# Attention and MLP kernel: one split for the last queries' transposes, the row sums' guard and reciprocal after their transpose

## The chip, the cores and the metric

One core of a Trainium2 chip runs the whole program. The metric is device microseconds (us) of that core. The kernel before took 748.15 us, the median of three runs (747.27 to 751.06 us).

## The reference

The inputs are q, k, v of 4 batches, 8 heads, 576 positions and 64 channels, a small MLP that gives a position bias, and the weights of a two-layer MLP. Cut to what matters:

```python
scores = scale * np.matmul(q, k.transpose(0, 1, 3, 2)) + bias
attn = np.exp(scores - np.max(scores, axis=-1, keepdims=True))
attn = attn / (np.sum(attn, axis=-1, keepdims=True) + 1e-09)
x = np.matmul(attn, v)                       # then to (2304, 512)
h = x @ w_in                                 # 512 -> 2048
g = np.where(h >= 1, h, np.where(h <= -1, 0, (h + 1) ** 2 / 4))
out = g @ w_out                              # 2048 -> 512
```

All is float32. The kernel gets this from TensorE by splitting each operand into a rounded part ("hi", or h) and the rest ("lo", or l), and multiplying the parts.

## The kernel before

The program has three stages: the bias table (to about 69 us in the trace), the attention (to about 349 us) and the MLP. Both edits lie in the attention.

The attention goes over 16 head pairs n = 0 to 15 (4 pairs of heads times 4 batches). Each pair has five blocks of queries, k = 0 to 4. Blocks 0 to 3 hold 128 queries for each of the two heads j; block 4, called L, holds the last 64 queries of both heads, stacked on the 128 partitions. For a block and head, TensorE makes the scores S (L455, L456; for L: L476, L477) into one of two PSUM buffers, VectorE adds the bias and finds the row's extreme in one custom operation (`e<-S,bias`, L458, for L: L478), and ScalarE takes the exponential and sums it into a column of the 128x9 tile `sum` (L465, L484).

Then `transposes` (L521, for L: L526) turns e with TensorE, 4 pieces into a PSUM bank T, and `split` writes hi and lo of it: ScalarE casts T to hi (L496) and VectorE subtracts (L497), or, for five of the eight blocks k < 4, ScalarE copies T (L501), GpSimd or VectorE casts (L503, L505) and GpSimd subtracts (L506). Block L is split in two halves of 256 columns, one for each head, both by ScalarE and VectorE. `shared` turns the rest of the columns (T_s). `values` multiplies by v (O, L559, L561) once after block 1 and once after block 4, 20 matmuls for each, and ScalarE copies O to x. T, O and R (below) share four PSUM banks.

After block L's exponential, ScalarE adds the guard 1e-9 to `sum` (L488). The step `inv` (L672) takes VectorE's reciprocal of it, 128x9. After the second `values` of the pair, `recips` (L545) transposes it into R, 9x128, ScalarE copies it to r (L547), and SyncE stores r (L548) into a DRAM tile rT. Later `scale_x` reads xT and rT back, adds the halves (L396) and multiplies by the reciprocals (L397) on VectorE.

The work of a pair's second half lags: its second `values` and `recips` are issued between the score blocks 2 of the next pair. The order within an engine is that of the program text, rearranged by the framework's scheduler by its own estimates wherever the code does not pin an instruction (`keep`, `pool`). SyncE's queue holds all DMA issues but a few, in order.

So around R the program has, on TensorE: the 20 matmuls of O for head pair n, then R, then the scores of blocks 2 and 3 of pair n + 1 with their transposes, then S_L. On VectorE: a cast `vs` (L178), which must wait for O's last matmul since it overwrites the v tile that O reads, then `e<-S,bias` of block 2, subtractions, and `e<-S,bias` of block 3. This place is called a joint below; there is one behind each R, 15 inside the attention and one at its end.

Of the kernel before, what the change touches and what calls it, by code (L numbers as in the profile page):

```python
# [12 lines left out]
AF = mybir.ActivationFunctionType  # L13
# [8 lines left out]
P = 128  # L22
# [25 lines left out]
def attn_cpb_moe_kernel(ctx, tc, qk, vL, cb, win, wout, lw, ident, ii, out):  # L48
    nc = tc.nc
# [367 lines left out]
    with ExitStack() as ph:  # L417
# [23 lines left out]
        def scores(n, k, qkv, bias):  # L441
            qs, q0, kh, kl = qkv["q"][:, 0], qkv["q"][:, 1], qkv["k"], qkv["l"]
            if k == 0:
                sums[n] = stp.tile([P, 9], F32, tag="sum", name=f"sum{n}", bufs=3)
            later = []
            sm = sums[n]
            mx = stp.tile([P, 2], F32, tag="mx", name=f"mx{n}_{k}", bufs=6)
            if k < 4:
                e = ep.tile([P, 2 * S], F32, tag="e", name=f"e{n}_{k}")
                for j in range(2):  # L450
                    ps = psS.tile([P, 2, 512], F32, tag="S", name=f"S{n}_{k}_{j}")
                    qc = slice(P * k, P * k + P) if j == 0 else slice(704 + P * k, 704 + P * k + P)
                    for hf in range(2):
                        kc = S * j + HS * hf
                        nc.tensor.matmul(ps[:, hf, :HS], qs[:, qc], kh[:, kc : kc + HS], start=True, stop=False)  # L455
                        nc.tensor.matmul(ps[:, hf, :HS], q0[:, qc], kl[:, kc : kc + HS], start=False, stop=True)  # L456
                    ev = e[:, S * j : S * j + S]
                    nc.vector.tensor_tensor_reduce(  # L458
                        out=ev.rearrange("p (a b) -> p a b", a=2),
                        in0=ps[:, :, :HS],  # L460
                        in1=bias[k][:, S * j : S * j + S].rearrange("p (a b) -> p a b", a=2),
                        scale=-0.125, scalar=BIG, op0=ALU.add, op1=ALU.min, accum_out=mx[:, j : j + 1],
                    )
                    later.append(
                        lambda ev=ev, j=j: nc.scalar.activation(  # L465
                            ev, ev, AF.Exp, bias=mx[:, j : j + 1], scale=-1.0, accum_out=sm[:, 4 * j + k : 4 * j + k + 1]
                        )
                    )
            else:
                e = ep.tile([P, S], F32, tag="eL", name=f"e{n}_L", bufs=2)  # L470
                ps = psS.tile([P, 2, 512], F32, tag="S", name=f"S{n}_L")
                for hf in range(2):
                    for j in range(2):
                        qc = slice(512 + D * j, 640 + D * j)
                        kc = 640 * j + HS * hf
                        nc.tensor.matmul(ps[:, hf, :HS], qs[:, qc], kh[:, kc : kc + HS], start=j == 0, stop=False)  # L476
                        nc.tensor.matmul(ps[:, hf, :HS], q0[:, qc], kl[:, kc : kc + HS], start=False, stop=j == 1)  # L477
                nc.vector.tensor_tensor_reduce(  # L478
                    out=e.rearrange("p (a b) -> p a b", a=2), in0=ps[:, :, :HS],
                    in1=bias[4].rearrange("p (a b) -> p a b", a=2),  # L480
                    scale=-0.125, scalar=BIG, op0=ALU.add, op1=ALU.min, accum_out=mx[:, 0:1],
                )
                def last():
                    y = nc.scalar.activation(e, e, AF.Exp, bias=mx[:, 0:1], scale=-1.0, accum_out=sm[:, 8:9])  # L484
                    for j in range(2):
                        h_ = slice(D * j, D * j + D)
                        nc.scalar.copy(diag[n % 2][h_, h_], e[h_, 512:S])
                    nc.scalar.activation(sm, sm, AF.Identity, bias=eps_s)  # L488
                    return y

                later.append(last)
            return e, later

# [15 lines left out]
        def EV(n, k, j):  # L509
            return nc.gpsimd if (k, j) in POOL and n < LASTP else None  # L510

        def transposes(n, k, es, eT):
            hi, lo = eT
            off = P * (k % 2)
            e = es[k]
            if k < 4:
                for j in range(2):
                    ps = psT.tile([P, 4, P], F32, tag="T", name=f"T{n}_{k}_{j}")
                    for tb in range(4):
                        c0 = 640 * j + P * tb  # L520
                        nc.tensor.transpose(ps[:, tb, :], e[:, c0 : c0 + P], id_s)  # L521
                    split(ps, hi[:, 4 * j : 4 * j + 4, off : off + P], lo[:, 4 * j : 4 * j + 4, off : off + P], EV(n, k, j), (k, j))
            else:
                ps = psT.tile([P, 4, 2, D], F32, tag="T", name=f"T{n}_L")
                for tb in range(4):
                    nc.tensor.transpose(ps[:, tb].rearrange("p a b -> p (a b)"), e[:, P * tb : P * tb + P], id_s)  # L526
                for j in range(2):
                    split(ps[:, :, j, :], hi[:, 4 * j : 4 * j + 4, 256:320], lo[:, 4 * j : 4 * j + 4, 256:320], EV(n, k, j), (k, j))

        def shared(n, half, es, eT):  # L530
            hi, lo = eT
# [8 lines left out]
        def recips(n):  # L540

            p, b = n // B, n % B
            sm = sums.pop(n)
            pr = psO.tile([P, 512], F32, tag="T", name=f"R{n}")
            nc.tensor.transpose(pr[:9, :P], sm, id_s)  # L545
            r = sp.tile([9, P], F32, tag="r", name=f"r{n}")
            nc.scalar.copy(r, pr[:9, :P])  # L547
            nc.sync.dma_start(out=rT[p][b].rearrange("(k q) -> k q", q=P), in_=r)  # L548

        def values(n, half, es, eT, vs):  # L550
# [79 lines left out]
        for n in range(N):  # L630
            p, b = n // B, n % B
            if n + 2 < N:
                preps[n + 2] = prep(n + 2)
            es[n] = []
            if n >= LASTP:
                go[0] = False
            for k in range(5):
                e, later = scores(n, k, qkv[n], bias[p])
                es[n].append(e)
                exps = [False]  # L640

                def exp_():
                    if not exps[0]:
                        exps[0] = True
                        for f in later:
                            exps.append(f())

                if CFG["ex"][k] == 0:
                    exp_()
                step(2 * k)  # L650
                if p + 1 < NP:
                    for k_ in range(5):
                        if (b, k) == LB[k_]:
                            with ExitStack() as after:
                                if p == 0 and k_ in (0, 1, 4):
                                    after.enter_context(tc.issue_after(copied[2].ins))
                                bias.setdefault(p + 1, {})[k_] = load_bias(p + 1, k_)

                def tr(n=n, k=k):
                    half = k // 2 if k < 4 else 1  # L660
                    if k in (0, 2):
                        w = 256 + D * half
                        eT[n, half] = (
                            (tp0, tp1)[half].tile([P, 9, w], F32R, tag=f"hi{half}", name=f"hi{n}_{half}"),
                            (tp0, tp1)[half].tile([P, 9, w], F32R, tag=f"lo{half}", name=f"lo{n}_{half}"),
                        )
                    transposes(n, k, es[n], eT[n, half])
                    if k in (1, 4):
                        shared(n, half, es[n], eT[n, half])

                def inv(n=n):
                    nc.vector.reciprocal(out=sums[n], in_=sums[n])  # L672

                def rc(n=n):
                    recips(n)

                if k in (1, 4):
                    def av(n=n, half=0 if k == 1 else 1):
                        values(n, half, es[n], eT[n, half], qkv[n]["v"])
                    queue.append([tr, inv] if k == 4 else [tr])  # L680
                    late.append([CFG["lag"][0 if k == 1 else 1], [av] if k == 1 else [av, rc]])
                else:
                    queue.append([tr])
                while late and late[0][0] <= 0:
                    queue.append(late.pop(0)[1])
                for x in late:
                    x[0] -= 1
                drain(CFG["dr"][k], exp_, CFG["ex"][k])
                exp_()
                step(2 * k + 1)  # L690
# [415 lines left out]
```

## Time and profile before

| | |
|---|---|
| median of three runs | 748.15 us (747.27, 748.15, 751.06) |
| profiled execution | span 749.8 us (no other time of this execution is given), 13722 instructions |
| busy over the span | PE 94%, PEld 83%, DVE 72%, ACT 69%, POOL 69% |
| chain that ended last | PE 64%, DVE 6%, DMA 6%, POOL 5%, ACT 5%, issue 3% |

PE is TensorE's matmuls, PEld its weight loads, DVE VectorE, ACT ScalarE, POOL GpSimd, SP SyncE. Shares over the whole span mix three stages. The distance between two R's is the time that one head pair costs. Durations of neighbours on an engine overlap a little, so that an instruction takes somewhat less room in a row of them than its duration.

### The profile page before, as it was taken

The numbers are of one execution on the slowest core, as the hardware profiler recorded it, in microseconds if no ns is written. First come the engines' busy times: TensorE is split into PE (matmuls) and PEld (weight loads), VectorE is DVE, ScalarE is ACT, GpSimd is POOL, SyncE is SP. The second block draws the span as 40 slices with busy tenths as digits, with TensorE's granted clock in tenths as the row PEclk, the third lists the DMA queues.
The fourth block names the chain that finished last, engine by engine and source line by source line (L and its number), as shares of the span: only waits on it lengthen the run. The fifth ranks groups of instructions, "written<-read, shape, count | busy, mean of one in ns | idle before, by whom it ended". The sixth has DMA issues, their size and how long they took to land.

```text
span 749.8 us, 13722 instructions
## 1 busy us (share of the span) xinstructions
PE 703.8 (94%) x4640; PEld 621.8 (83%) x4640; DVE 537.5 (72%) x1043; ACT 518.8 (69%) x1156; POOL 519.1 (69%) x440
## 2 busy tenths in 40 slices
PE   4687999899999999989999999999999999999997
PEld 1234999888888898989988898989899988888886
DVE  7899888868898888886877776354455465666653
ACT  8896989869888998986656565344444547666563
POOL 9887778858878888871757677565656545665662
PEclk9899999989999999999999999999999999999999
DMA  8887799996997797744364645023021002000002
GB/s 228 231 271 228 200 249 240 238 234 167 233 275 192 186 271 190 177 121 162 95 199 135 197 147 163 35 83 90 7 63 32 1 1 84 1 1 1 0 1 85
DMA packets 58662, 103.37 MB, mean 138 GB/s; under 512 B 12496, under 2 KB 32736, under 8 KB 58592
## 3 DMA queue, kind: packets, MB, share of 16 engines
q1 hardware_dynamic: 56000, 92.31, 43.5%
q0 software_dynamic: 2304, 9.96, 6.4%
q8 instruction: 37, 0.61, 0.3%
q14 instruction: 33, 0.27, 0.1%
q10 hardware_dynamic: 288, 0.22, 0.1%
HBM read 67.38 MB, written 25.12 MB: 123 GB/s over the span
## 4 chain that ended last, share of the span: by engine, by line
PE 64%; DVE 6%; DMA 6%; POOL 5%; ACT 5%; issue 3%; SPq 1%; DVEq 0%; ACTq 0%; POOLq 0%
PE y L716 23%; PE h L716 16%; PE p L716 7%; PE O L559 5%; PE T L521 3%; PE S L455 3%; DMA kh<-kh 2%; PE S L456 2%; POOL lo L506 2%; DVE e L458 2%; PE O L561 1%; DMA v<-in_vL_dram 1%; ACT e L465 1%; POOL ls L136 1%; DMA x<-rT 1%
## 5 line engine op out<-in xcount | busy, mean ns | idle before, releaser
L958 POOL TENSOR_TENSOR gl<-c,gh 128x384 fp32r<-128x384 f32 x64 | 70.8, 1107 | 104.9 <-issue 87.5
L506 POOL TENSOR_TENSOR lo<-c,hi 128x512 fp32r<-128x512 f32 x75 | 101.4, 1368 | 30.2 <-DVE hi L505 27.7
L716 PE MATMUL y<-w1h,gl 128*128 128x512 f32 x288 | 114.0, 396 | 0.0
L716 PE MATMUL y<-w1l,gh 128*128 128x512 f32 x288 | 113.7, 395 | 0.0
L716 PE MATMUL y<-w1h,gh 128*128 128x512 f32 x288 | 112.0, 389 | 0.0
L465 ACT ACTIVATE e<-e,mx 128x576 f32<-128x576 f32 x128 | 100.5, 789 | 15.4 <-DVE mx L458 15.3
L458 DVE CUSTOM_DVE_ANT_0 e<-S,bias 128x576 f32<-128x576 f32 x128 | 94.4, 749 | 18.7 <-PE S L456 18.2
L455 PE MATMUL S<-kh,qa 128*128 128x288 f32 x256 | 80.0, 329 | 10.0 <-DVE mx L458 5.5
L776 ACT ACTIVATE c<-c,half_s 128x384 f32<-128x384 f32 x64 | 39.4, 615 | 60.7 <-DVE c L773 60.7
L456 PE MATMUL S<-ls,qa 128*128 128x288 f32 x256 | 73.6, 305 | 0.0
L521 PE MATMUL T<-id_s,e 128*128 128x128 f32 x512 | 71.6, 276 | 1.3 <-DVE lo L497 0.8
L982 POOL TENSOR_TENSOR gl<-c,gh 128x384 fp32r<-128x384 f32 x32 | 32.7, 1022 | 47.8 <-issue 22.3
L716 PEld LDWEIGHTS y<-w1h,gl 128*128 128x128 f32 x288 | 54.0, 187 | 11.5
L521 PEld LDWEIGHTS T<-id_s,e 128*128 128x128 f32 x512 | 59.4, 143 | 4.1 <-DVE lo L497 1.2
L455 PEld LDWEIGHTS S<-kh,qa 128*128 128x128 f32 x256 | 49.2, 192 | 15.4 <-DVE mx L458 8.8
L284 ACT ACTIVATE u<-lw,nthr 128x576 f16<-128x576 f32 (+17 forms) x104 | 57.8, 647 | 5.5 <-PE B L303 3.0
L716 PEld LDWEIGHTS y<-w1l,gh 128*128 128x128 f32 x288 | 54.0, 187 | 8.0
L716 PEld LDWEIGHTS y<-w1h,gh 128*128 128x128 f32 x288 | 54.1, 188 | 7.7
L303 PEld LDWEIGHTS <-qh 128*32 128x32 f16 x704 | 19.4, 101 | 49.4 <-issue 21.1
L286 POOL TENSOR_SCALAR u<-lw,thr 128x576 f16<-128x576 f32 (+17 forms) x36 | 51.6, 1448 | 5.0 <-PE B L303 3.8
L779 DVE TENSOR_TENSOR c<-h,c 128x384 f32<-128x384 f32 x64 | 35.4, 554 | 26.8 <-ACT c L776 26.0
L954 ACT CAST gh<-c 128x384 fp32r<-128x384 f32 x64 | 32.9, 514 | 30.5 <-DVE c L779 28.6
(266 smaller groups left out, 2112.7 us busy)
## 6 DMA issues: line engine op xcount, KB each, us to landing
bias_d<-y SPq DMA_DIRECT2D x36, 295.5 KB
qk<-in_qk_dram SPq DMA_DIRECT2D x16, 608.0 KB
qa<-in_qk_dram POOLq DMA_DIRECT2D x16, 608.0 KB, 7.2
x<-xT SPq DMA_DIRECT2D x48, 192.0 KB
raw<-in_win_dram SPq DMA_DIRECT2D x16, 512.0 KB
raw<-in_wout_dram SPq DMA_DIRECT2D x16, 512.0 KB
v<-in_vL_dram SPq DMA_DIRECT2D x16, 320.0 KB
qa<-ls SPq DMA_DIRECT2D x32, 152.0 KB
```

The lines of the kernel that those rows point to most:

```text
L284: tc.keep_in_program_order(nc.scalar.activation(u[:, :n_], lw1[:, :n_], AF.Sigmoid, bias=nthr[:, m : m + 1], scale=STEEP))
L286: EN[x].tensor_scalar(out=u[:, :n_], in0=lw1[:, :n_], scalar1=thr[:, m : m + 1], scalar2=None, op0=ALU.is_gt)
L455: nc.tensor.matmul(ps[:, hf, :HS], qs[:, qc], kh[:, kc : kc + HS], start=True, stop=False)
L456: nc.tensor.matmul(ps[:, hf, :HS], q0[:, qc], kl[:, kc : kc + HS], start=False, stop=True)
L458: nc.vector.tensor_tensor_reduce(out=ev.rearrange("p (a b) -> p a b", a=2), in0=ps[:, :, :HS], in1=bias[k][:, S * j : S * j + S].rearrange ...
L465: lambda ev=ev, j=j: nc.scalar.activation(ev, ev, AF.Exp, bias=mx[:, j : j + 1], scale=-1.0, accum_out=sm[:, 4 * j + k : 4 * j + k + 1])
L506: r = nc.gpsimd.tensor_tensor(out=lo, in0=m, in1=hi.bitcast(F32), op=ALU.subtract)
L521: nc.tensor.transpose(ps[:, tb, :], e[:, c0 : c0 + P], id_s)
L559: nc.tensor.matmul(ps[:, :w], vs[:, 4 * j + tb, :], src[:, 4 * j + tb, :], start=first and tb == 0, stop=False)
L716: a = nc.tensor.matmul(out, w, x, start=start, stop=stop)
L776: keep(nc.scalar.activation(c, c, AF.Square, scale=0.5, bias=half_s))
L958: keep(nc.gpsimd.tensor_tensor(out=gl, in0=c, in1=gh.bitcast(F32), op=ALU.subtract))
```

## The change

Block L's bank is split by one ScalarE cast and one VectorE subtraction of 512 columns in place of two each of 256. The guard is added by ScalarE in the operation that copies R out of PSUM (9x128), in place of an operation of its own on the 128x9 tile. The reciprocal is taken behind that on VectorE, of the 9x128 tile r instead of the 128x9 tile `sum`, with ScalarE's result before it and the store behind it.

```diff
-                    nc.scalar.activation(sm, sm, AF.Identity, bias=eps_s)
                     return y
...
-                for j in range(2):
-                    split(ps[:, :, j, :], hi[:, 4 * j : 4 * j + 4, 256:320], lo[:, 4 * j : 4 * j + 4, 256:320], EV(n, k, j), (k, j))
+                split(ps, *[t[:, :8, 256:320].rearrange("p (j t) d -> p t j d", j=2) for t in (hi, lo)])
...
-            nc.scalar.copy(r, pr[:9, :P])
+            nc.scalar.activation(r, pr[:9, :P], AF.Identity, bias=eps_s[:9])
+            nc.vector.reciprocal(out=r, in_=r)
             nc.sync.dma_start(out=rT[p][b].rearrange("(k q) -> k q", q=P), in_=r)
...
-                def inv(n=n):
-                    nc.vector.reciprocal(out=sums[n], in_=sums[n])
-
...
-                    queue.append([tr, inv] if k == 4 else [tr])
+                    queue.append([tr])
```

VectorE at the joint behind R of pair 8 (about 231.6 us in the trace). Before, where `a10` is a weight's bit operation (L116) and the rows run from the reciprocal of pair 8, of which three rows on are left out, to the subtractions of pair 9's block 1:

```order
L672 RECIPROCAL sum8_3509<-sum8_3509 128x9
...
L497 TENSOR_TENSOR lo8_1_3696<-T8_L_3829,hi8_1_3695 128x4x64
L497 TENSOR_TENSOR lo9_0_3848<-T9_0_0_3849,hi9_0_3847 128x4x128
L178 CAST vs10_3987<-v10_3802 128x10x64
L458 ISA e9_2_3901,mx9_2_3900<-S9_2_1_3908,bias2_2_3394 128x576
...
L116 SCALAR_TENSOR_TENSOR a10_3896<-a10_3896,raw10_3760 128x512
L458 ISA e9_3_3940,mx9_3_3939<-S9_3_0_3941,bias2_3_3433 128x576
...
L121 CAST w0h1_1495<-a10_3896 128x512
L497 TENSOR_TENSOR lo9_0_3848<-T9_1_0_3918,hi9_0_3847 128x4x128
```

The same engine and place now:

```order
L496 TENSOR_TENSOR lo9_0_3820<-T9_0_0_3821,hi9_0_3819 128x4x128
L178 CAST vs10_3960<-v10_3777 128x10x64
L458 ISA e9_2_3874,mx9_2_3873<-S9_2_1_3881,bias2_2_3373 128x576
...
L546 RECIPROCAL r8_3864<-r8_3864 9x128
L116 SCALAR_TENSOR_TENSOR a10_3869<-a10_3869,raw10_3735 128x512
L458 ISA e9_3_3913,mx9_3_3912<-S9_3_0_3914,bias2_3_3412 128x576
...
L121 CAST w0h1_1495<-a10_3869 128x512
L496 TENSOR_TENSOR lo9_0_3820<-T9_1_0_3891,hi9_0_3819 128x4x128
```

The reciprocal has moved from ahead of block 1's scores to between `e<-S,bias` of block 2 and of block 3, behind the cast `vs`; the second subtraction of T_L is gone from ahead of `vs`.

VectorE at the joint behind R of pair 11 (about 282.4 us), where `x0_2_0` is a block of attention output that is read back and scaled (L396, L397). Before:

```order
L497 TENSOR_TENSOR lo12_0_4623<-T12_0_0_4624,hi12_0_4622 128x4x128
L396 TENSOR_TENSOR x0_2_0_4504<-x0_2_0_4504 128x384
L397 TENSOR_TENSOR x0_2_0_4504<-x0_2_0_4504,xr0_2_0_4505 128x384
L178 CAST vs13_4771<-v13_4581 128x10x64
L458 ISA e12_2_4675,mx12_2_4674<-S12_2_1_4682,bias3_2_4427 128x576
...
L497 TENSOR_TENSOR lo12_0_4623<-T12_1_0_4693,hi12_0_4622 128x4x128
L497 TENSOR_TENSOR lo12_0_4623<-T12_1_1_4700,hi12_0_4622 128x4x128
L458 ISA e12_3_4724,mx12_3_4723<-S12_3_0_4725,bias3_3_4466 128x576
```

Now:

```order
L178 CAST vs13_4735<-v13_4547 128x10x64
L458 ISA e12_2_4639,mx12_2_4638<-S12_2_1_4646,bias3_2_4394 128x576
...
L546 RECIPROCAL r11_4630<-r11_4630 9x128
L396 TENSOR_TENSOR x0_2_0_4471<-x0_2_0_4471 128x384
L496 TENSOR_TENSOR lo12_0_4586<-T12_1_0_4657,hi12_0_4585 128x4x128
L397 TENSOR_TENSOR x0_2_0_4471<-x0_2_0_4471,xr0_2_0_4472 128x384
L496 TENSOR_TENSOR lo12_0_4586<-T12_1_1_4664,hi12_0_4585 128x4x128
L496 TENSOR_TENSOR lo12_0_4586<-T12_s0_4671,hi12_0_4585 128x256
L458 ISA e12_3_4688,mx12_3_4687<-S12_3_0_4689,bias3_3_4433 128x576
```

The two scaling operations have moved from ahead of `vs` to behind the reciprocal, and with one more subtraction they now stand between the scores of blocks 2 and 3. The same happens at the joints behind R of pairs 3 and 7.

## Rows read from the trace of the kernel before

**Rows 1.** The page, part 1: busy us, share of span, instructions.

```profile
PE 703.8 (94%) x4640; PEld 621.8 (83%) x4640; DVE 537.5 (72%) x1043; ACT 518.8 (69%) x1156; POOL 519.1 (69%) x440
```

**Rows 2.** Busy time by window, one head pair each, R to R.

```profile
core 0: us, PE busy (x) PEld busy (x) DVE busy (x) ACT busy (x) POOL busy (x), PEclk, DMA share, GB/s
...
231.60:249.20 17.60, 16.45 (x127) 15.51 (x125) 16.01 (x35) 15.54 (x40) 14.28 (x13) 1.00 0.73 193
```

**Rows 3.** Waits of PEld, 92 to 352 us: total us, times, longest.

```profile
PEld S L455 <- DVE mx L458: 7.3, 14, 1.6
PEld S_L L476 <- DVE mx L458: 3.8, 9, 1.4
...
PEld T L521 <- DVE lo L497: 1.2, 2, 0.6
```

**Rows 4.** Waits of DVE, 92 to 352 us.

```profile
DVE e L458 <- PE S L456: 17.6, 27, 3.2
DVE vs L178 <- PE O L561: 10.8, 11, 1.3
```

**Rows 5.** DVE by tile or line: ns min/median/max, first and last start, forms.

```profile
L257 DVE RECIPROCAL rsc<-m x1: 163/163/163, 6.6 to 6.6; 128x1 f32<-128x1 f32 x1
...
L672 DVE RECIPROCAL sum<-sum x16: 197/209/215, 89.4 to 345.5; 128x9 f32<-128x9 f32 x16
...
L497 DVE TENSOR_TENSOR lo<-T,hi x53: 673/680/694, 75.5 to 344.0; 128x512 fp32r<-128x512 f32 x53
...
L497 DVE TENSOR_TENSOR lo<-T_L,hi x32: 411/420/425, 88.6 to 346.7; 128x256 fp32r<-128x256 f32 x32
```

**Rows 6.** ACT by tile: the guard, the copy of R, the casts.

```profile
L488 ACT ACTIVATE sum<-sum,eps_s x16: 303/303/306, 84.4 to 345.2; 128x9 f32<-128x9 f32 x16
...
L547 ACT COPY r<-R x16: 250/250/251, 93.1 to 349.4; 9x128 f32<-9x128 f32 x16
...
L496 ACT CAST hi<-T x53: 559/587/610, 74.8 to 343.3; 128x512 fp32r<-128x512 f32 x53
...
L496 ACT CAST hi<-T_L x32: 348/370/389, 87.1 to 346.3; 128x256 fp32r<-128x256 f32 x32
```

**Rows 7.** DVE in order of time at pair 8's joint: start, us, idle before.

```profile
231.81 1.07 DVE L178 CAST vs<-v 128x640 fp32r<-128x640 f32 x1 [1.07 <-PE O L561]
232.80 0.74 DVE L458 CUSTOM_DVE_ANT_0 e<-S,bias 128x576 f32<-128x576 f32 x1
...
233.66 1.61 DVE L116 SCALAR_TENSOR_TENSOR a<-a,raw 128x512 int32<-128x512 int32 x1
235.19 0.74 DVE L458 CUSTOM_DVE_ANT_0 e<-S,bias 128x576 f32<-128x576 f32 x1
...
236.20 1.28 DVE L497 TENSOR_TENSOR lo<-T,hi 128x512 fp32r<-128x512 f32 x2
```

**Rows 8.** PE in order of time at the same joint.

```profile
234.24 0.60 PE L521 MATMUL T<-id_s,e 128*128 128x128 f32 x4
235.99 0.40 PE L476 MATMUL S_L<-kh,qa 128*128 128x288 f32 x1 [1.15 <-DVE mx L458]
```

**Rows 9.** DVE, then PE, in order of time at pair 11's joint.

```profile
281.56 0.77 DVE L396 TENSOR_TENSOR x<-x 128x384 f32<-128x384 f32 x1
282.36 1.73 DVE L397 TENSOR_TENSOR x<-x,xr 128x384 f32<-128x384 f32 x1
284.02 0.89 DVE L178 CAST vs<-v 128x640 fp32r<-128x640 f32 x1
284.83 0.74 DVE L458 CUSTOM_DVE_ANT_0 e<-S,bias 128x576 f32<-128x576 f32 x1
...
285.64 0.40 PE L455 MATMUL S<-kh,qa 128*128 128x288 f32 x1 [1.20 <-DVE mx L458]
```

**Rows 10.** DVE at the end of the attention.

```profile
349.85 0.56 DVE L773 TENSOR_SCALAR c<-h 128x384 f32<-128x384 f32 x1 [2.77 <-PE h L716]
```

**Rows 11.** Waits of PE, 92 to 352 us.

```profile
PE S L455 <- DMA kh<-kh: 3.4, 2, 2.0
```

## The prediction

> **What bounds the kernel now.** I read the page's busy shares first [rows 1]: TensorE's matmuls are busy for 94% of the span, VectorE, the next engine, for 72%. That is a mean over three stages, so I went to the attention, where both edits lie, and read one head pair from R to R [rows 2]. There TensorE is still ahead (16.45 of 17.60 us), but VectorE (16.01) and ScalarE (15.54) are close behind, and TensorE's granted clock is 1.00, the 2.4 GHz level. An engine that is busy 91% of a stretch can set the end wherever its work is bunched, so the next view is that of the waits. TensorE's weight loads wait for VectorE's `mx`, the result of `e<-S,bias`, 14 times at S and 9 times at S_L, together 11.1 us, and twice for a subtraction [rows 3]. VectorE for its part waits for TensorE at `vs`, 11 times and 10.8 us, because `vs` overwrites what the O matmuls read [rows 4].
>
> The two fit together in time. During O TensorE is fed and VectorE runs dry; when O ends, VectorE has a heap of work at once, and TensorE soon hangs on it. In pair 8's joint `vs` starts after 1.07 us of idling, and from there on VectorE has no gap worth naming until 236.20, while TensorE stands for 1.15 us before S_L until `e<-S,bias` of 235.19 is done [rows 7, 8]. So behind R VectorE sets the end, and in the run-up to O TensorE does.
>
> **The change part by part.** *The reciprocal.* Sixteen of 128x9 go, each 209 ns; sixteen of 9x128 come. A partition more or less is no work for VectorE that a row here shows; the elements behind each partition count, and these go from 9 to 128. One element took 163 ns, nine took 209 [rows 5]: 46 ns for 8 elements, 5.75 ns each. So 128 take 163 + 127 x 5.75 = 893 ns. Bounds: if the elements went as fast as those of a subtraction, (680 - 420) / 256 = 1.0 ns each [rows 5], it would be 163 + 130 = 293 ns; with the longest of the sixteen, (215 - 163) / 8 = 6.5 ns, 989 ns. I take 0.89 us, since both ends of its slope are reciprocals. Two subtractions in a row of 1.28 us [rows 7] against 0.68 for one show that a neighbour overlaps by 0.08 us, so the room that it takes is 0.81 us (0.21 to 0.91).
>
> The Trainium skill, "VectorE: DVE Perf Modes", the section on the fixed hardware budget in the walkthrough of the pipeline, says that the reciprocal is an iterated divide with a repeat count of 8. Eight cycles at the 0.96 GHz that the skill's first page ("Trainium Kernel Development and Optimization", Hardware Hierarchy) gives would be an estimated 8.3 ns for each element, so 1.22 us, dearer than the 5.75 ns of the rows make it; by that rule the sum below would end some 4 us higher. I go by the rows.
>
> Where it stands matters more than its size. Before, it was in the run-up to O, where the time is TensorE's. Now it stands at nearly every joint between `e<-S,bias` of block 2 and that of block 3, in the stretch in which TensorE waits for VectorE. It also waits for R and for ScalarE's copy, but `vs` and `e` occupy VectorE for 0.99 + 0.75 us behind O's end [rows 7], and R is one short matmul behind O, its copy 0.25 us [rows 6]: r is there by then, unless ScalarE is late. Behind it in VectorE's queue are subtractions that release transposes' banks, and `e` of block 3, for which S_L waits.
>
> The twelve joints without a scaling operation: full pass-through would be 0.81 us each, none would be 0. The 23 waits over 15 joints say that about each joint has one that VectorE ends, but many are short, 11.1 / 23 = 0.48 us on average, so some slack goes first; and at some joints the scheduler now puts `e` of block 3 ahead of one 0.60 us subtraction, which spares S_L what the transposes then get. I take 0.6: 12 x 0.81 x 0.6 = +5.8 us.
>
> *The three joints with scaling* (pairs 3, 7, 11). Before, L396 and L397 began during O, and `vs` could start only behind them, at 284.02; TensorE paid 1.20 us for block 2's `e` at 285.64 [rows 9]. Now `vs` does not wait for them, which gives up to 1.2 us back, but both operations stand with the reciprocal ahead of block 3's `e`, for 0.77 + 1.73 us by these rows, or some 1.5 us if the second is as short as the first. Net: +0.3 to +1.3 us beside the reciprocal; I take +0.5, nearer to the short end, since the long L397 is one row. With 0.81 each, 3 x 1.3 = +3.9 us.
>
> *The pieces that go.* On VectorE two subtractions of 420 ns become one of about 680: 0.16 us, and the old reciprocal's room, 0.13 us [rows 5]. On ScalarE the guard goes, 0.30 us, two casts of 370 become one of 587: 0.15, and the copy of R (250 ns) may grow to the guard's kind of operation, by at most 0.05 + 0.08 us from the rows' differences [rows 6]; about 0.35 us. All this lies in the run-up to O, hidden beside matmuls. If each pair gains 0.15 us of TensorE's small waits there: -2.4 us; bounds 0 and, if all of VectorE's 0.29 counts, -4.6.
>
> *Transfers.* No DMA is added. The store of r now waits for VectorE too, but the store of x's second half now goes ahead of it in SyncE's queue, so what is queued behind it (loads that are read a pair later) is delayed less than that. TensorE waits for `kh` transfers 3.4 us in two places [rows 11], and a late TensorE loses some of that: -1.3 us for the joints ahead of the longer one.
>
> *The end.* The sixteenth reciprocal stands ahead of the MLP's first clamp, where VectorE had idled for 2.77 us [rows 10]; so it can delay the clamp by no more than its room, 0.81 us, while the old one stood ahead of the last subtractions and goes. The two I set against each other.
>
> Sum: 5.8 + 3.9 - 2.4 - 1.3 = +6.0 us on the span of 749.8, so 755.8. That span is 1.65 us above the median of the runs; against the median 748.15 it gives 754.2 us.
>
> **The rivals.** *Absorbed.* VectorE's own waits, 10.8 us at `vs` and 17.6 at the scores [rows 4], show slack in each pair. If a joint passes on only 0.3 of the reciprocal, the sum is 12 x 0.24 + 3 x 0.8 - 2.4 - 1.3 = +1.6: 749.7 us, within 0.5%. For it: VectorE is busy for 16.01 of a pair's 17.60 us, so 1.6 us of it are free [rows 2]. Against it: the slack lies ahead of `vs`, the new work behind it.
>
> *Faster: the reciprocal is cheap.* If the slope is that of a subtraction, its room is 0.21 us against the 0.13 that goes; it decides if the 9x128 form takes under some 0.4 us. Then VectorE and ScalarE are both lighter in each pair by about 0.2 and 0.35 us, and with 0.28 us for each of 15 pairs the time is 748.15 - 4.2 = 744 us. For it: the two engines are near TensorE in each pair [rows 2]. Against it: 46 ns more for eight elements.
>
> *Dearer.* If an element costs half as much again as the slope (a slope from one 128x1 row is weak, since its fixed part may differ), room is 1.2 us and the nine joints' worth of pass-through (12 x 0.6 + 3 = 10.2) adds 10.2 x 0.37 = 3.8: 758 us. The skill's count of 8 named above is this case.
>
> **How the numbers follow.** Forecast 0.55, dearer 0.08, absorbed 0.25, faster 0.12. What a measurement of this kernel can tell from no change is about 0.5%, 3.7 us: between 744.4 and 751.9. The forecast's own range is 750.5 to 759, from pass-through 0.35 to 1. For 8 in 10 I go from 747.5, which takes in the absorbed case, to 761, which takes in the dearer one. Slower 0.55 + 0.08 = 0.63, same 0.25, faster 0.12.
>
> **What would show it.** Right: L546's reciprocal at 0.8 to 1.0 us; more waits of S_L and T for VectorE behind R; R to R longer by 0.3 to 0.6 us in ordinary pairs, by over 1 us in the pairs behind joints 3, 7 and 11; the MLP unchanged. Wrong: a reciprocal under 0.4 us; R to R equal or shorter although the reciprocal is long, which would put the bound elsewhere than at VectorE; or a loss in SyncE's queue (waits of L199 for r), which I have priced at nothing.

## The result and the profile after

The kernel after takes 753.53 us, the median of five runs (752.91 to 754.55), against 747.62 us for the kernel before beside it (747.27 to 751.06): a ratio of 1.0074, 95% interval 1.0056 to 1.0092. It is slower by 5.9 us in the medians; by the ratio it is 5.5 us, 4.2 to 6.9. The profiled execution of after took 754.55 us, with a span of 752.5.

The page of after, part 1 (busy us, share of the span, instructions), answers to [rows 1]:

```profile
PE 709.9 (94%) x4640; PEld 621.9 (83%) x4640; DVE 546.2 (73%) x1027; ACT 517.7 (69%) x1124; POOL 518.0 (69%) x440
```

VectorE has 16 instructions fewer and 8.7 us more. TensorE runs the same 4,640 matmuls and shows 6.1 us more busy time: a matmul that TensorE takes at a lower clock counts as busy too, so I read the loss from time stamps and not from idle time.

The operations that changed, in after, by tile: ns min/median/max, first and last start, form (compare [rows 5, 6]):

```profile
L545 ACT ACTIVATE r<-R,eps_s x16: 352/354/359, 94.2 to 352.5; 9x128 f32<-9x128 f32 x16
L546 DVE RECIPROCAL r<-r x16: 932/936/941, 94.6 to 352.8; 9x128 f32<-9x128 f32 x16
...
L495 ACT CAST hi<-T_L x16: 561/564/587, 88.4 to 348.1; 128x512 fp32r<-128x512 f32 x16
...
L496 DVE TENSOR_TENSOR lo<-T_L,hi x16: 678/692/692, 89.9 to 348.7; 128x512 fp32r<-128x512 f32 x16
```

The reciprocal takes 936 ns. Now where the time is lost. R is one matmul for each head pair, and its starts mark the pairs. Of before I take a second profiled execution here (e0, 744.9 us, span 743.1), since in the first a wait for `kh` and a granted clock of 0.58 behind it (150 to 155 us) belong to that execution alone. Rows of R by tile, of this one and of after:

```profile
L545 PE MATMUL R<-id_s,sum x16: 271/271/271, 92.7 to 342.6; 128*9 128x128 f32 x16
```

```profile
L543 PE MATMUL R<-id_s,sum x16: 271/271/271, 93.7 to 351.8; 128*9 128x128 f32 x16
```

The sixteenth R comes 9.2 us later, and behind it both need the same time (743.1 - 342.6 = 400.5; 752.5 - 351.8 = 400.7): the MLP lost nothing. Start to start of R, in us, column n is from pair n to pair n + 1 and so holds the joint behind pair n:

```
pair          0    1    2    3    4    5    6    7    8    9   10   11   12   13   14
before      15.2 16.2 16.0 17.2 17.6 17.3 16.1 17.0 17.6 17.3 16.1 17.0 17.4 18.6 13.3
after       15.5 16.9 16.7 17.9 17.9 17.3 16.2 18.0 17.9 17.3 16.2 18.0 18.5 20.1 13.7
```

This execution of before was a quick one (744.9 us against a median of 746.74 us on its chip), so the differences say where, and the medians how much.

**An ordinary joint.** VectorE of after at the joint behind pair 8, in order of time (start, us, idle before it), answers to [rows 7]:

```profile
230.33 1.30 DVE L178 CAST vs<-v 128x640 fp32r<-128x640 f32 x1 [0.97 <-PE O L560]
...
231.55 0.74 DVE L458 CUSTOM_DVE_ANT_0 e<-S,bias 128x576 f32<-128x576 f32 x1
...
232.23 0.94 DVE L546 RECIPROCAL r<-r 9x128 f32<-9x128 f32 x1
233.09 0.92 DVE L116 SCALAR_TENSOR_TENSOR a<-a,raw 128x512 int32<-128x512 int32 x1
233.94 0.74 DVE L458 CUSTOM_DVE_ANT_0 e<-S,bias 128x576 f32<-128x576 f32 x1
```

TensorE there, answers to [rows 8]:

```profile
234.75 0.41 PE L476 MATMUL S_L<-kh,qa 128*128 128x288 f32 x1 [1.16 <-DVE mx L458]
```

The reciprocal stands where the forecast put it, but block 3's `e` starts 3.61 us after `vs`, against 3.38 before: L116 took 0.92 us here and 1.61 there, and most of the reciprocal's time came out of that. The pair lost only 0.3 us.

What L116 waits out can be read from GpSimd's rows: it has a subtraction at the same time, before and after.

```profile
233.43 1.28 POOL L506 TENSOR_TENSOR lo<-c,hi 128x512 fp32r<-128x512 f32 x1
```

```profile
232.18 1.29 POOL L505 TENSOR_TENSOR lo<-c,hi 128x512 fp32r<-128x512 f32 x1
```

L116 ends at 235.27 before and at 234.01 in after, 0.56 and 0.54 us behind the end of that subtraction (234.71 and 233.47), although it began 0.23 and 0.91 us behind its start. Where no such subtraction ran beside it, at joint 4 of the first profile of before, L116 took 0.68 us:

```profile
165.10 0.68 DVE L116 SCALAR_TENSOR_TENSOR a<-a,raw 128x512 int32<-128x512 int32 x1
```

The reciprocal keeps its 0.94 us inside the subtraction. So at this joint it ran in time in which L116 would have stood; the rows show this, but not why.

**A joint with scaling.** VectorE of after behind pair 11, answers to [rows 9]:

```profile
281.71 1.31 DVE L178 CAST vs<-v 128x640 fp32r<-128x640 f32 x1 [0.98 <-PE O L560]
282.95 0.74 DVE L458 CUSTOM_DVE_ANT_0 e<-S,bias 128x576 f32<-128x576 f32 x1
...
283.62 0.94 DVE L546 RECIPROCAL r<-r 9x128 f32<-9x128 f32 x1
284.49 0.79 DVE L396 TENSOR_TENSOR x<-x 128x384 f32<-128x384 f32 x1
285.20 0.68 DVE L496 TENSOR_TENSOR lo<-T,hi 128x512 fp32r<-128x512 f32 x1
285.80 0.54 DVE L397 TENSOR_TENSOR x<-x,xr 128x384 f32<-128x384 f32 x1
286.27 0.68 DVE L496 TENSOR_TENSOR lo<-T,hi 128x512 fp32r<-128x512 f32 x1
286.87 0.41 DVE L496 TENSOR_TENSOR lo<-T_s,hi 128x256 fp32r<-128x256 f32 x1
287.20 0.74 DVE L458 CUSTOM_DVE_ANT_0 e<-S,bias 128x576 f32<-128x576 f32 x1
```

and TensorE there:

```profile
286.02 0.63 PE L520 MATMUL T<-id_s,e 128*128 128x128 f32 x4 [1.04 <-DVE lo L496]
```

The wait for block 2's `e` (1.20 us in [rows 9]) is gone, and a wait of 1.04 us for a subtraction behind the reciprocal and the scaling is there instead. e3 below shows that the reciprocal's length has no part in it.

**Pair 13, and the clock.** The largest difference, 1.5 us, is not VectorE's alone. TensorE of after in the run-up to the O of pair 14, then the first and the last rows of that O, and R:

```profile
333.63 1.40 PE L558 MATMUL O<-hi,vs 128*128 128x320 f32 x4 [1.46 <-DVE lo L496]
...
338.01 0.31 PE L560 MATMUL O<-lo,vs 128*128 128x320 f32 x1
338.15 0.27 PE L543 MATMUL R<-id_s,sum 128*9 128x128 f32 x1
```

and two windows there (length, busy of PE, PEld, DVE, ACT, POOL, granted clock, DMA share, GB/s):

```profile
330.00:334.00 4.00, 2.01 (x12) 1.57 (x12) 4.00 (x7) 2.52 (x6) 3.92 (x5) 0.94 0.62 176
334.00:338.00 4.00, 4.00 (x19) 4.00 (x19) 2.43 (x6) 2.48 (x8) 0.99 (x2) 0.63 0.32 99
```

TensorE was busy for half of the first window, waited 1.46 us, and the granted clock then fell: 0.63 is a mix of the 2.4 and the 1.2 GHz level. The twenty matmuls take 338.15 - 333.63 = 4.52 us. One experiment below (e7) has the same wait of 1.46 us without the fall, and there they take 333.11 - 330.10 = 3.01 us. So this 1.5 us is the clock's. It is not of one execution alone: the profiles of e6, e1, e2 and e8 have a fall at the same O, behind waits of 1.46 to 1.59 us, and 20.1 to 20.2 us for this pair. Those of e3, e4, e7, e10, e11 and e12 and both of before pass waits of 1.46 to 1.60 us there without one. A second fall stands ahead of the attention's first pairs:

```profile
68.00:72.00 4.00, 2.44 (x24) 1.88 (x24) 3.79 (x8) 0.00 (x0) 1.85 (x2) 0.84 0.72 207
72.00:76.00 4.00, 3.87 (x19) 3.27 (x19) 3.17 (x10) 1.68 (x4) 0.00 (x0) 0.73 1.02 300
```

It makes the first R 1.0 us late: the seven profiles of this case with a fall there have that R at 93.4 us or later, the six without at 92.8 or earlier. This one does not go with the change, since e10, the kernel before without its guard, has it and e3 and e8 do not. Without the two, after's attention is 9.24 - 0.95 - 1.51 = 6.8 us longer than that of before's quick execution.

### The profile page after: what moved, and what is told of

It is laid out like the page before. It is cut to its first block, busy times and chain, and to the rows that moved or that the text cites. A ratio compares the mean times of both kernels' runs of the same rounds, so it can differ in the third digit from the quotient of the medians.

```text
span 752.5 us, 13692 instructions
## 1 busy us (share of the span) xinstructions
PE 709.9 (94%) x4640; PEld 621.9 (83%) x4640; DVE 546.2 (73%) x1027; ACT 517.7 (69%) x1124; POOL 518.0 (69%) x440
## 4 chain that ended last, share of the span: by engine, by line
PE 61%; DVE 8%; ACT 7%; DMA 5%; POOL 4%; issue 4%; SPq 2%; DVEq 0%; ACTq 0%; POOLq 0%
PE y L712 25%; PE h L712 17%; PE p L712 7%; PE O L558 5%; DMA bias<-bias_d 3%; ACT e L465 3%; POOL lo L505 2%; PE T L520 2%; DVE e L458 2%; DVE lo L496 1%; ACT c L500 1%; PE O L560 1%; PE S L455 1%; PE S L456 1%; DVE hi L504 1%
## 5 line engine op out<-in xcount | busy, mean ns | idle before, releaser
L520 PE MATMUL T<-id_s,e 128*128 128x128 f32 x512 | 74.0, 276 | 5.6 <-DVE lo L496 4.2
```

## The experiments

All are compared with the kernel before on the same chip; intervals are 95%, and a difference in us is worked out from the ratios. The full change, run again there, was e6:

> The full change once more, beside the next three on one chip, since the time of the kernel before spread by 7 us on the chip of the first three experiments: ratio 1.005 to 1.009.

It measured 754.38 us, ratio 1.0086 (1.0059 to 1.0113): the loss holds. A profile of the kernel before, again, was e0:

> The kernel before again, for a second profile: the first one spends 23.1 us between the R of pairs 3 and 4 with a wait for kh transfers, where its neighbours spend 16 to 17. If that wait belongs to one execution, the distance here is 17 to 18 us; if to the kernel, 22 us or more.

It is the kernel before of the table above. From R of pair 3 to that of pair 4 it takes 17.2 us, so the wait of the first profile belongs to that execution.

**The parts apart.** e1 is the kernel before with the single split only:

```diff
-                for j in range(2):
-                    split(ps[:, :, j, :], hi[...256:320], lo[...256:320], EV(n, k, j), (k, j))
+                split(ps, *[t[:, :8, 256:320].rearrange("p (j t) d -> p t j d", j=2) for t in (hi, lo)])
```

> Only block L's split is merged; guard and reciprocal stay as before. Size theory (the longer reciprocal behind R is the loss): within 1 us of the kernel before or up to 2.4 us faster (ratio 0.997 to 1.001), as the run-up to O gains 0.15 us of small waits per pair at most. Order theory (the scheduler's new order, above all on TensorE and in the split, is the loss): slower by 2 us or more (ratio over 1.003), since this edit alone already moves 126 rows on TensorE.

e2 is after with the old two splits, so only guard and reciprocal move:

> Only the guard and the reciprocal are moved behind R; block L is split in two as before. Size theory: as slow as the full change or up to 2 us slower still (ratio 1.006 to 1.011), R to R longer as in the full change. Theory that the merged split is the loss: within 1 us of before (ratio 0.999 to 1.001).

e1 measured 754.94 us, 1.0127 (1.0075 to 1.0178), e2 752.34 us, 1.0064 (1.0035 to 1.0092). e2 shows that moving the guard and the reciprocal by itself loses nearly all. e1 missed the size theory's range and lies in that of the order theory: the edit that takes instructions away was the dearer one. Its waits of TensorE (total us, times, longest) and one of them:

```profile
PE S L455 <- DMA kh<-kh: 6.9, 4, 3.6
```

```profile
200.54 0.37 PE L455 MATMUL S<-kh,qa 128*128 128x288 f32 x1 [3.56 <-DMA kh<-kh]
```

In its schedule the next pair's S stands ahead of O matmuls and waits for a transfer that after's profile, with the same split, never waits for. So e1 measures a placement along with the split. How much of its loss this wait makes in every execution is open, since the first profile of before also has a wait for `kh` that e0 has not.

**The guard's removal alone.** e10 is before without L488.

```diff
-                    nc.scalar.activation(sm, sm, AF.Identity, bias=eps_s)
```

> The kernel before without the guard of 1e-9 on the row sums (left out; the sums are at least 1, where it is below float32's step). One ScalarE operation of 0.30 us less per pair, in the run-up to O. Prediction's pricing (0.15 us per pair for all that goes there): 0 to 2 us faster (ratio 0.997 to 1.000). Order theory (any edit reshuffles the schedule, and a reshuffle costs): slower, ratio over 1.002.

It measured 746.66 us against 746.74, 0.9997 (0.9981 to 1.0013): 0.30 us less of ScalarE in each pair gave nothing that can be told from zero (a gain of 1.4 us to a loss of 1.0 by the interval).

**The size.** e3 is the full change with a reciprocal of nine of the 128 columns, in nearly the same order:

```diff
-            nc.vector.reciprocal(out=r, in_=r)
+            nc.vector.reciprocal(out=r[:, :9], in_=r[:, :9])
```

> The full change, but the reciprocal takes 9 of the 128 columns of r (the other 119 row sums stay sums, so the output is scaled wrongly): VectorE's order is that of the full change but for one cast, with an operation of about 0.2 us in place of 0.94 us. Size theory: the loss goes, within 1.5 us of before (ratio 0.997 to 1.002). Order and wait theory (the place behind ScalarE's copy, the scaling operations moved behind vs): at least 3 of the 5.9 us stay (ratio 1.004 or more).

e4 issues the full reciprocal three times in a row:

```diff
             nc.vector.reciprocal(out=r, in_=r)
+            nc.vector.reciprocal(out=r, in_=r)
+            nc.vector.reciprocal(out=r, in_=r)
```

> The full change with three reciprocals in a row (the value comes out the same), so 2 x about 0.86 = 1.7 us more behind each R. Size theory with the slack used up by the first: 0.8 to 1 of it passes, 16 x 1.7 x 0.9 = 24 us more than the full change (ratio 1.030 to 1.045). Theory that slack of about 2 us per pair takes most of it: under 10 us more (ratio under 1.02).

The reciprocal in e3, by tile:

```profile
L546 DVE RECIPROCAL r<-r x16: 194/198/203, 93.6 to 347.2; 9x9 f32<-9x9 f32 x16
```

e3 measured 749.09 us, 1.0034 (1.0010 to 1.0058): 2.5 us over before instead of 6.4 in e6. So 738 ns less in each of sixteen places, 11.8 us of work, give back 3.9 us, a third (the two intervals together allow 1.2 to 6.6 us). That lies between the ranges of both theories. Some of it can be the clock, since e3's profile has neither of the two falls. Behind joints 4, 7, 8 and 11 e3's pairs are only 0 to 0.2 us shorter than after's, behind joint 3 the pair is 0.4 longer. At joint 8 L116 and at joint 11 L396 take up the room, up to the end of GpSimd's subtraction, and TensorE's wait behind joint 11 is the same 1.04 us (two rows of joint 8, then two of joint 11):

```profile
229.37 1.67 DVE L116 SCALAR_TENSOR_TENSOR a<-a,raw 128x512 int32<-128x512 int32 x1
```

```profile
229.20 1.29 POOL L505 TENSOR_TENSOR lo<-c,hi 128x512 fp32r<-128x512 f32 x1
```

```profile
280.22 1.54 DVE L396 TENSOR_TENSOR x<-x 128x384 f32<-128x384 f32 x1
```

```profile
282.50 0.63 PE L520 MATMUL T<-id_s,e 128*128 128x128 f32 x4 [1.04 <-DVE lo L496]
```

e4 measured 775.88 us, 1.0385 (1.0357 to 1.0414), 22.4 us over e6. Each added reciprocal fills 0.94 - 0.08 = 0.86 us, so 32 of them are 27.5 us, of which 0.81 comes through; part of that is the clock's, which falls in e4's profile at 172, 192 and 268 us too. The first reciprocal had slack to eat; the second and third found little left.

**The place.** e7 keeps the full reciprocal and issues those of pairs 0 to 11 one pair later, behind a score of block 2, so that they run while TensorE is at O:

```diff
-            nc.vector.reciprocal(out=r, in_=r)
-            nc.sync.dma_start(out=rT[p][b].rearrange("(k q) -> k q", q=P), in_=r)
+            def rest():
+                nc.vector.reciprocal(out=r, in_=r)
+                nc.sync.dma_start(out=rT[p][b].rearrange("(k q) -> k q", q=P), in_=r)
+            owed.append(rest)
+            while owed and n > 11:
+                owed.pop(0)()
...
+                    if (k, j) == (2, 0) and len(owed) > 1:
+                        with tc.issue_after(y.ins):
+                            owed.pop(0)()
```

> The full change, but the 9x128 reciprocals of pairs 0 to 11 are issued one pair later, just ahead of vs, where VectorE waits for the O matmuls; those of pairs 12 to 15 stay. As many reciprocals of the same length. Place theory (the loss is the reciprocal in the stretch behind R): ratio 0.996 to 1.003. Theory that 0.94 us more on VectorE cost the same wherever they stand: ratio 1.005 to 1.009.

VectorE of e7 ahead of the joint behind pair 8:

```profile
224.57 0.94 DVE L553 RECIPROCAL r<-r 9x128 f32<-9x128 f32 x1
225.43 0.61 DVE L501 TENSOR_TENSOR lo<-T,hi 128x512 fp32r<-128x512 f32 x1
...
226.93 1.34 DVE L178 CAST vs<-v 128x640 fp32r<-128x640 f32 x1 [0.88 <-PE O L571]
228.19 0.74 DVE L460 CUSTOM_DVE_ANT_0 e<-S,bias 128x576 f32<-128x576 f32 x1
```

e7 measured 748.71 us, 1.0015 (0.9999 to 1.0032). The reciprocals are as long as before, VectorE still idles 0.88 us ahead of `vs`, and 5.3 us of e6's 6.4 are gone (3.0 to 7.6 by the two intervals). That is in the range of the place theory and below that of the other. But it is not shown that the reciprocal's own place makes the difference, since the edit moves more than that. At joints 3, 7 and 11 e7's L396 stands ahead of `vs` again, and L397 ahead of block 2's `e`:

```profile
141.10 0.53 DVE L396 TENSOR_TENSOR x<-x 128x384 f32<-128x384 f32 x1
```

R to R behind these three is 16.8, 16.8 and 17.3 us, together 3.0 less than in after. Pair 13 gives 1.5 back, which is the clock's: e7's profile lacks the fall at pair 14.

```profile
330.10 0.82 PE L569 MATMUL O<-hi,vs 128*128 128x320 f32 x4 [1.46 <-DVE lo L501]
...
333.11 0.27 PE L548 MATMUL R<-id_s,sum 128*9 128x128 f32 x1
```

The ordinary joints 0 to 10, where the reciprocal moved away and no scaling stands, give back 0.3 us in the sum (1.3 at joint 1; joints 2 and 10 are 0.3 and 1.0 longer).

e11 is e7 with the old two splits:

> The delayed reciprocals of e7_late, but block L split in two as before. If the single split gains in the run-up: 0 to 2 us slower than e7_late's ratio of 1.0015 (1.001 to 1.004). If the single split costs, as e1_split's 1.0127 suggests for its schedule: faster than e7_late, ratio 0.993 to 1.000.

It measured 749.55 us, 1.0037 (1.0019 to 1.0055). Here the single split is worth 0.0022, while between e2 and e6 the sign is the other way; both differences lie inside the intervals.

**The scaling operations.** e8 is the full change with the scaling of pairs 3, 7 and 11 planned a step earlier, so that it leaves the joint; e12 makes the same edit to the kernel before:

```diff
-XQ = {(0, 0): (39, "raw", 43), (1, 0): (79, "raw", 83), (2, 0): (118, "raw", 123), ...
+XQ = {(0, 0): (39, "raw", 42), (1, 0): (79, "raw", 82), (2, 0): (118, "raw", 122), ...
```

> The full change, with the scaling operations of three joints issued one step earlier, so that they stand ahead of vs again; the reciprocals stay behind R. If the moved scaling costs 0.5 us per joint as the prediction took it: 1 to 2 us less than the full change in the same call (ratio lower by 0.001 to 0.003). If it costs nothing: the same within 1 us.

> The kernel before with the scaling operations of three joints issued one step earlier. In e8_xearly the head pairs at two of these joints took 16.5 us from R to R, in the kernel before 17.2 and 17.3: if that is the scaling ahead of vs, 3 x 0.8 = 2.4 us faster than before (ratio 0.995 to 0.999). If it came with e8_xearly's other order: no change (0.999 to 1.002).

e8 measured 749.97 us, 1.0039 (1.0021 to 1.0056), 3.5 us less than e6 by the ratios. R to R of e8 behind joints 3, 7 and 11 is 16.0, 16.5 and 16.5 us, 1.9, 1.5 and 1.5 less than after; the pairs ahead of them, which now hold the scaling, give 1.1, 0.2 and 0.2 back. This is more than the 1 to 2 us that were expected. e12 measured 750.57 us, 1.0054 (1.0031 to 1.0078): in the kernel before the same edit costs 4.0 us, where a gain or no change was expected. Its waits of TensorE, and VectorE ahead of the longest of them:

```profile
PE O L559 <- DVE lo L497: 7.8, 6, 2.4
```

```profile
206.21 1.64 DVE L396 TENSOR_TENSOR x<-x 128x384 f32<-128x384 f32 x1
207.77 0.41 DVE L497 TENSOR_TENSOR lo<-T_L,hi 128x256 fp32r<-128x256 f32 x1
208.10 1.49 DVE L397 TENSOR_TENSOR x<-x,xr 128x384 f32<-128x384 f32 x1
209.51 0.48 DVE L497 TENSOR_TENSOR lo<-T_s,hi 128x320 fp32r<-128x320 f32 x1
209.91 0.74 DVE L458 CUSTOM_DVE_ANT_0 e<-S,bias 128x576 f32<-128x576 f32 x1
210.59 0.41 DVE L497 TENSOR_TENSOR lo<-T_L,hi 128x256 fp32r<-128x256 f32 x1
```

The scaling stands there ahead of and between the subtractions of T_L and T_s, and O's wait of 2.4 us, until 210.14, ends with that of T_s. The clock falls behind that wait (0.71 from 208 to 212 us), so part of the cost is the clock's. In after the edit pays, in the kernel before it costs; the two differ in the split and in the reciprocal's place, and which of them decides is not shown. No version was faster than the kernel before beyond its interval.

## Why the prediction was right, and where its terms were off

The forecast was +6.0 us, and +5.9 was measured; the direction holds, and so does the edit that was to cause it. That the sum came out within 0.1 us is luck: its terms were off, and their errors cancel.

**The reciprocal's duration** was put at 893 ns and is 936: from 128x9 of before, (936 - 209) / 119 = 6.1 ns for each element behind a partition, where 5.75 was taken. The Trainium skill's count of 8 ("VectorE: DVE Perf Modes", First, the fixed hardware budget) made an estimated 1.22 us; the trace does not agree with that. By the prediction's own pass-through that estimate would have added 0.33 x 10.2 = 3.3 us, not some 4. The cheap and the dear rival are both out.

**Its place** is as forecast, and e2 shows that moving it there costs. The forecast named as its sign more waits of S_L and T for VectorE. Those of T came: in after TensorE waits 4.2 us in 8 places for `lo` there, against 0.8 in 2 of e0:

```profile
PE T L520 <- DVE lo L496: 4.2, 8, 1.0
```

```profile
PE T L521 <- DVE lo L497: 0.8, 2, 0.4
```

S_L's did not (2.3 us in 2 places, against 2.6 in 3), and the waits of weight loads at S even fell, from 7.3 us [rows 3] to 2.8. The waits of T are the scaling's more than the reciprocal's: with a short reciprocal (e3) they are 3.9 us in 5 places, with the scaling moved away (e8) 1.2 in 5.

**The pass-through** of 0.6 was the term with the least behind it, and too high at the ordinary joints. "R to R longer by 0.3 to 0.6 us in ordinary pairs" is true of a mean only: the differences are 0 to 0.3 behind joints 5, 6, 8, 9 and 10, 0.7 to 0.8 behind 1 and 2, and 1.1 behind 12, where VectorE of after has no gap from 300.95 to 316.8 us. The twelve took 4.1 us beside the 1.5 of the clock, where 12 x 0.49 = 5.8 was forecast; with the -2.4 of the pieces that go the forecast is 3.4, but no run shows that gain. The 23 waits from which the forecast took the pass-through are those of weight loads; the matmuls of before waited for `mx` in 8 places, 6.3 us. Joint 9 shows where it went. VectorE of e0 and then of after, at block 2's and 3's `e`:

```profile
245.02 0.76 DVE L458 CUSTOM_DVE_ANT_0 e<-S,bias 128x576 f32<-128x576 f32 x1 [0.49 <-PE S L456]
```

```profile
249.56 0.93 DVE L546 RECIPROCAL r<-r 9x128 f32<-9x128 f32 x1
250.42 0.68 DVE L458 CUSTOM_DVE_ANT_0 e<-S,bias 128x576 f32<-128x576 f32 x1
```

Before, VectorE idled 0.49 us ahead of an `e`; now the reciprocal fills that gap. At joints 4 and 8 L116 gave way, as seen above. The absorbed rival, 0.3 a joint, was the nearer one here: e3's 3.9 us of 11.8 is 0.33.

**The scaling joints** were put at +3.9 and show 0.7, 1.0 and 1.0, so 2.7 us. The wait given back and the new one are both seen above. The sum has the reciprocal there at its full 0.81 us each, and this step was wrong in kind: e3, with a reciprocal of 0.20 us, has the same wait of 1.04 us and R to R as long (18.3, 17.8 and 17.9 us against 17.9, 18.0 and 18.0). e8 shows what costs there, the scaling operations: moving them alone gave back 3.5 us.

**The pieces that go** were put at -2.4 us, and no run shows that gain. e10 has nothing for the guard, within its interval. For the split no run gives a clean number: e1 and e2 against e6 have it costing, e11 against e7 has it saving, as the order around it differs; the old reciprocal's room was not tested alone.

**Transfers** (-1.3) cannot be settled. TensorE waits for no `kh` in after's profile, but also for none in e0's, so the 3.4 us of [rows 11] belong to one execution. SyncE's queue, priced at nothing, stands for VectorE at the store of r (L547) 4.5 us in 9 places between 92 and 353 us, 1.2 at longest, and once 0.4 us at L200. TensorE waits for no transfer in after's profile, so no loss from it shows.

**The end** is as forecast: 400.5 and 400.7 us behind the last R, though the clamp behind the last reciprocal starts 1.9 us behind R, where it started 1.0 behind it before: TensorE lost 0.2 us of that at most.

**Not in the prediction** was the clock: 2.5 us of after's profiled execution. So a saving that no run shows and a clock loss that was not priced stand against terms that were too large. How much of the 5.9 us of the medians is the clock's stays open in part: e6's profile has both falls again, e3's neither. The runs' mean granted clocks speak against a large share: the four runs of after and e6 at 0.993 to 0.995 took 751.3 to 753.5 us, those of the kernel before at these clocks, on the three chips of the experiments, 743.7 to 747.8. Open too is what the order on TensorE, which every edit here changed, has in the sum.

## What to carry to other kernels

Price an operation by what its engine does at its new place, not by its engine's share of busy time: here shortening an operation by 0.74 us gave back a third of that, and what was added to it cost four fifths. Where the order is a scheduler's, test an edit in both surroundings before giving it a sign: the same earlier scaling came out with opposite signs, and for the split no sign could be had. Look for idle time joint by joint; a mean pass-through hid joints that took nothing and joints that took all. And before an operation's new place is called the cause, see what else the scheduler moved with it: two scaling operations here.

## What the runs showed of the hardware

VectorE's reciprocal goes by the elements behind a partition, not by the partitions: 163 ns for 128x1, 198 for 9x9, 209 for 128x9, 936 for 9x128, some 6.1 ns each. ScalarE's copy of 9x128 from PSUM took 250 ns as a copy and 354 with a bias added, 0.10 more, at the upper end of what was allowed for. Two VectorE operations ended by the end of GpSimd's subtraction and not by their own length: L116, 0.68 us alone, took 0.92 to 1.67 us and ended 0.54 to 0.56 us behind it at joint 8 of before, after and e3, and L396 ended 0.41 and 0.42 us behind it at joint 11 of after and e3 (the subtractions end at 284.87 and 281.34). The reciprocal beside it took its 0.94 us. And the granted clock can fall in the middle of the attention, behind a stretch in which TensorE waited, and cost as much as the wait: 1.5 us behind one of 1.46 us. In five profiles the fall came there and in eight not; why is open.
